# One raw PSUM tensor with up to three score slots, one bit group for both halves of a block, and new priorities

## The chip, the core and the metric

The kernel runs on one core of one Trainium2 chip (trn2). The metric is the device time of one execution in microseconds (us). The profile's span is about 2 us shorter in most runs, and 4 us shorter in the run that the prediction was made from, because it goes from the first to the last instruction. Fast and slow executions are kept apart; every comparison here is between fast runs, and every profile line that is quoted comes from a profile of the fast state.

## The reference

Hash attention over 32 heads (batch 4, 8 heads, 768 positions, head size 64), then a channel mix on the joined heads.

```python
# attention: positions see each other only if their 6 hash bits agree
q_bits = einsum('bhsd,dk->bhsk', q, proj) > 0          # the same for k
mask   = q_bucket[..., :, None] == k_bucket[..., None, :]
attn   = softmax(where(mask, q @ k.T / sqrt(64), -1e9))
x      = (attn @ v), heads joined to [4, 768, 512]
# channel mix with a shift by one position
xk = mu_k * x + (1 - mu_k) * x_prev                    # xr with mu_r
k  = relu(xk @ w_k) ** 2                               # 512 -> 1024
out = sigmoid(xr @ w_r) * (k @ w_v)                    # 1024 -> 512
```

## The kernel before

The kernel works on 16 blocks, each a pair of heads. A block goes through these steps:

- SyncE (SP) issues the loads of q, k and v.
- VectorE (DVE) splits q and k into a high and a low half-precision part.
- A transposing DMA turns them. For the first two blocks TensorE (PE) does this.
- TensorE forms six bucket bits for each position.
- VectorE reads the signs, and four small DMAs ("rows") lay the bits beside q and k as extra rows.
- Nine steps of scores, 128 x 1024 each, go through PSUM to ScalarE (ACT), which takes the exp.
- Attention times v follows, then the normalisation on VectorE, a transpose and the shift mix.

After every four blocks a batch is complete and its channel mix can run (groups KP, R and V below). From block 4 on, v is centred: GpSimd (POOL) sums it and a small "mean" matmul follows.

All work is entered in a list with an estimated duration, a priority and its dependencies. A planner in Python then simulates five engines and a DMA queue, and picks at each moment the ready operation of the lowest priority number. The order that comes out is fixed in the program. Each engine goes through its list in that order; a trace below shows an engine standing 3.0 us at one instruction while the ones behind it wait. The priorities count in blocks: an operation of block n has priority n + PR[name].

```python
LAG = {"PE": 0.30, "ACT": 0.25, "DVE": 0.20, "POOL": 0.20, "SP": 1.8, "GQ": 2.0}   # us, the planner's own numbers
PR = {
    'ldq': -2.811, 'ldv': -2.337, 'hi': -5.393, 'lo': -1.084, 'tr': -2.122, ...   # 34 numbers
    'va': 0.273, 'vsum': -2.003, 'mean': -0.515, ...
}
class Plan:
    def schedule(self):            # (cut) list scheduling
        ...
                    if o.take is not None:
                        cls, name, moe = o.take
                        if not avail[cls] or (moe and moe_held[cls] >= self.slots[cls][1]):
                            skipped.append(item)      # no PSUM slot free by the plan: try another
                            continue
        ...
# PSUM: two score slots of two banks, four small slots of one bank
sc_t = [psum.tile([P, STEP], FP32, name=f"sc{i}", tag=f"sc{i}") for i in range(2)]     # STEP = 1024
sm_t = [psum.tile([P, 512], FP32, name=f"sm{i}", tag=f"sm{i}") for i in range(4)]
plan = Plan({"sc": (2, 2), "sm": (4, 3)})
...
for h in range(2):                 # bits of a block: two groups of 384 columns, one small slot each
    def f(nm=nm, h=h):
        ps = sm(nm)
        for w_, st in ((p1, True), (p2, False)):
            for i in its:          # q and k of two heads, on four column strips
                nc.tensor.matmul(ps[32 * i : 32 * i + 32, 0:HALF], w_, a[:, i // 2, h * HALF : (h + 1) * HALF],
                                 start=st, stop=not st)
    def g(nm=nm, h=h):             # VectorE takes the sign bits
        nc.vector.tensor_scalar(out=bx_t[sx][lo_p:P, h * HALF : (h + 1) * HALF].bitcast(U16), in0=sm(nm)[...], ...)
```

The softmax here doesn't subtract the row's maximum and nothing guards it: scores larger than these inputs give would overflow.

## Time and profile before

The kernel took 260.83 us (two runs, 260.77 and 260.90).

The lines below are the busy time of each engine and the page's 40 equal slices of the span, in tenths of busy time, for the kernel before.

```profile
PE 239.3 (93%) x2519; PEld 143.5 (56%) x2519; DVE 195.1 (76%) x391; ACT 185.5 (72%) x242; POOL 57.9 (23%) x98
...
PE   6768898888999999999999989999999999999994
```

The busy time by stretch, kernel before. The columns are the stretch, its length, then the busy time and the instruction count of each engine, the granted clock of TensorE, the share of the 16 DMA engines and the DMA rate.

```profile
16.00:32.00 16.00, 13.11 (x154) 7.36 (x154) 13.47 (x25) 10.90 (x13) 6.60 (x11) 0.89 0.85 152
48.00:64.00 16.00, 13.24 (x183) 8.63 (x181) 12.81 (x23) 14.14 (x16) 7.58 (x13) 1.00 1.04 172
...
80.00:96.00 16.00, 15.84 (x141) 8.36 (x139) 15.62 (x28) 10.52 (x15) 5.23 (x6) 1.00 0.67 165
112.00:128.00 16.00, 16.00 (x194) 9.64 (x191) 14.85 (x31) 13.26 (x17) 2.75 (x4) 1.00 0.87 249
```

There are two stages. Up to about 64 us TensorE has gaps, because no channel-mix matmul can start before the first batch's attention is done. After that, TensorE is busy for practically the whole of each stretch.

The waits of TensorE, kernel before (who waited for whom: us in total, times, longest):

```profile
PE sc L553 <- ACT pt L557: 4.5, 11, 0.7
PE sm L420 <- DVE qh L405: 1.3, 1, 1.3
PE sm L443 <- DVE ak L422: 1.3, 2, 0.7
...
PE sm L681 <- DVE ob L599: 1.1, 1, 1.1
...
PE sm L609 <- DVE ob L599: 0.3, 1, 0.3
```

The largest is 4.5 us, scores waiting for a slot that exp has not yet emptied. Two more lines of the kernel before are needed later (start, duration, what). The first is from SyncE's timeline, the issue of a load of v; the second is from the chain of work in order of time, GpSimd's first sum of that v.

```profile
47.90 0.40 SPq L339 DMA_DIRECT2D vn<-in_v_dram  x1
```

### The profile page before, as it was taken

The page shows a single profiled execution, that of the slowest core. Times are in us where ns is not written, and L with a number is a line of the kernel's source. Part 1 is how long each engine was busy: PE and PEld are TensorE (multiplying, and loading weights), DVE is VectorE, ACT ScalarE, POOL GpSimd, SP SyncE. Part 2 cuts the span into 40 slices and gives each one's busy share as a digit, 9 for nine tenths or more (in the row PEclk, how much of TensorE's full clock was granted, in tenths as well). Part 3 has the DMA queues.
Part 4 walks back from the last instruction along what each step waited for, and adds up shares of the span by engine and source line. Part 5 has one row for each costly group of instructions (what it writes and reads, how often), then busy time and mean ns, then how long its engine had stood idle before and what let it go on. Part 6 is the DMA issues. An engine that isn't in the chain of part 4 may idle for free.

```text
span 256.8 us, 6319 instructions
## 1 busy us (share of the span) xinstructions
PE 239.3 (93%) x2519; PEld 143.5 (56%) x2519; DVE 195.1 (76%) x391; ACT 185.5 (72%) x242; POOL 57.9 (23%) x98
## 2 busy tenths in 40 slices
PE   6768898888999999999999989999999999999994
PEld 2334564555666456656666655555666666555441
DVE  4999676777789997989998999898685753675322
ACT  3838888888994598878898967586798986147320
POOL 2491415056051330504041424040000000000000
PEclk9998999999999999999999999999999999999999
DMA  6968979799998479796978987888200011220132
GB/s 191 382 168 155 163 174 172 199 171 180 225 201 227 116 199 175 212 241 190 274 148 266 216 241 149 233 164 166 89 3 6 3 41 43 82 86 1 41 123 82
DMA packets 64565, 39.78 MB, mean 155 GB/s; under 512 B 46756, under 2 KB 60952, under 8 KB 64536
## 3 DMA queue, kind: packets, MB, share of 16 engines
q1 hardware_dynamic: 62248, 36.76, 58.4%
q0 software_dynamic: 2208, 2.62, 6.3%
q8 instruction: 19, 0.31, 0.5%
q14 instruction: 10, 0.08, 0.1%
q10 hardware_dynamic: 80, 0.00, 0.0%
HBM read 24.12 MB, written 6.29 MB: 118 GB/s over the span
## 4 chain that ended last, share of the span: by engine, by line
PE 63%; DMA 15%; DVE 10%; POOL 3%; SPq 3%; issue 2%; ACT 2%; POOLq 0%; DVEq 0%
PE sc L553 16%; PE sm L681 15%; PE sm L652 11%; PE sm L583 10%; DMA vn<-in_v_dram 8%; PE sm L671 7%; PE sm L443 4%; DMA qn<-in_q_dram 3%; DMA ak<-kh 2%; POOL vt L360 2%; DMA kn<-in_k_dram 2%; PE sm L609 2%; ACT pt L557 2%; SPq L334 1%; DVE xk L635 1%
## 5 line engine op out<-in xcount | busy, mean ns | idle before, releaser
L557 ACT ACTIVATE pt<-sc 128x1024 bf16<-128x1024 f32 x144 | 143.2, 1028 | 29.9 <-PE sc L553 28.3
L553 PE MATMUL sc<-aq,ak 128*128 128x512 f16 (+1 forms) x384 | 84.6, 329 | 4.5 <-ACT pt L557 4.5
L553 PEld LDWEIGHTS <-ak 128*128 128x128 f16 x384 | 33.6, 98 | 31.1 <-issue 12.2
L652 PE MATMUL sm<-xk,wk 128*128 128x384 bf16 x256 | 48.9, 326 | 0.2
L681 PE MATMUL sm<-wv,k 128*128 128x512 bf16 x192 | 47.8, 379 | 1.1 <-DVE ob L599 1.1
L583 PEld LDWEIGHTS <-pt 128*128 128x128 bf16 x1152 | 42.9, 97 | 9.0 <-issue 0.6
L583 PE MATMUL sm<-va,pt 128*128 128x65 bf16 x1152 | 44.6, 193 | 0.0
L656 ACT ACTIVATE kr<-sm 128x384 bf16<-128x384 f32 x64 | 31.3, 498 | 9.5 <-PE sm L652 7.5
L652 PEld LDWEIGHTS <-wk 128*128 128x128 bf16 x256 | 24.1, 98 | 15.2 <-issue 0.3
L360 POOL TENSOR_TENSOR vt<-vn 128x384 f32<-128x384 f32 x12 | 15.1, 1256 | 71.5 <-DMA vn<-in_v_dram 71.5
L659 DVE TENSOR_TENSOR k<-kr 128x384 bf16<-128x384 bf16 x64 | 23.8, 385 | 8.5 <-ACT kr L656 8.4
L674 ACT ACTIVATE rs<-sm 128x512 f32<-128x512 f32 x24 | 14.4, 599 | 22.1 <-PE sm L671 18.9
L681 PEld LDWEIGHTS <-k 128*128 128x128 bf16 x192 | 18.4, 98 | 19.5 <-issue 1.3
L688 DVE SCALAR_TENSOR_TENSOR os<-rs,sm 128x512 f32<-128x512 f32 x24 | 16.3, 684 | 16.5 <-PE sm L681 16.4
L671 PE MATMUL sm<-wr,xr 128*128 128x512 bf16 x96 | 24.6, 379 | 0.0
L619 POOL COPY xt<-xt 128x127 bf16<-128x127 bf16 x16 | 8.4, 525 | 69.1 <-DVE xt L615 64.4
L447 DVE TENSOR_SCALAR bx<-sm 128x384 uint16<-128x384 uint16 (+1 forms) x32 | 16.4, 549 | 3.3 <-PE sm L443 2.6
L599 DVE TENSOR_TENSOR ob<-sm,rc 128x384 bf16<-128x384 f32 x32 | 17.8, 556 | 0.9
L405 DVE SCALAR_TENSOR_TENSOR kh<-kn,kh 128x768 f16<-128x768 f32 x15 | 18.3, 1219 | 0.1
L635 DVE SCALAR_TENSOR_TENSOR xk<-df,muk,xt 128x768 bf16<-128x768 bf16 x16 | 16.7, 1046 | 0.3
L443 PE MATMUL sm<-ak,p 128*32 128x384 f16 x124 | 14.4, 335 | 2.3 <-DVE ak L422 1.3
L635 DVE SCALAR_TENSOR_TENSOR xr<-df,mur,xt 128x768 bf16<-128x768 bf16 x16 | 16.1, 1018 | 0.0
(76 smaller groups left out, 195.3 us busy)
## 6 DMA issues: line engine op xcount, KB each, us to landing
vn<-in_v_dram SPq DMA_DIRECT2D x16, 384.0 KB
out_dram<-os SPq DMA_DIRECT2D x24, 256.0 KB
qn<-in_q_dram SPq DMA_DIRECT2D x15, 384.0 KB
kn<-in_k_dram SPq DMA_DIRECT2D x15, 384.0 KB
wk<-in_moe_w_k_dram POOLq DMA_DIRECT2D x4, 256.0 KB, 5.3
wv<-in_moe_w_v_dram POOLq DMA_DIRECT2D x4, 256.0 KB, 8.7
wr<-in_moe_w_r_dram POOLq DMA_DIRECT2D x2, 256.0 KB, 5.4
aq<-bx SPq DMA_DIRECT2D x31, 9.0 KB
```

Of the source, the lines that this page charges most:

```text
L360: nc.gpsimd.tensor_tensor(out=vt[:, :, :, 0:E], in0=src[:, :, 0:3, 0:E], in1=src[:, :, 3:6, 0:E], op=ALU.add)
L405: nc.vector.scalar_tensor_tensor(out=nh[:, :, D:P], in0=nat.rearrange("p j (c d) -> p (j c) d", d=D), scalar=QS, in1=nh[:, :, 0:D], op0=AL ...
L443: nc.tensor.matmul(ps[32 * i : 32 * i + 32, 0:HALF], w_, a[:, i // 2, h * HALF : (h + 1) * HALF], start=st, stop=not st)
L553: nc.tensor.matmul(ps[:, lo - s * STEP : hi - s * STEP], side_a["k"][sa][:, j, jc * P : (jc + 1) * P], side_a["q"][sa][:, j, q0 : q0 + hi ...
L557: nc.scalar.activation(out=pt_t[sp][:, s * STEP : (s + 1) * STEP], in_=sc_t[plan.slot[nm]], func=AF.Exp, bias=EBIAS, scale=ESC)
L583: nc.tensor.matmul(oo[:, ic * 65 : ic * 65 + 65], pt_t[sp][:, o : o + P], va_t[sa][:, j, jc, 0 : D + 1], start=(not uc and ic == 0 and jc ...
L635: nc.vector.scalar_tensor_tensor(out=dst[smx], in0=df_t[sd], scalar=mu[:, t : t + 1], in1=x, op0=ALU.mult, op1=ALU.add)
L652: nc.tensor.matmul(ps[:, 0:HALF], wk_sb[:, d, fc * P : (fc + 1) * P], xk_t[mx[d]][:, h * HALF : (h + 1) * HALF], start=(d == 0), stop=(d = ...
L656: nc.scalar.activation(out=kr_t[sk], in_=sm(nm)[:, 0:HALF], func=AF.Relu, scale=0.5 ** 0.5)
L659: nc.vector.tensor_tensor(out=k2_t[s2][:, h * HALF : (h + 1) * HALF], in0=kr_t[sk], in1=kr_t[sk], op=ALU.mult)
L671: nc.tensor.matmul(sm(nr), xr_t[mx[d]][:, c * P : (c + 1) * P], wr_sb[:, d, :], start=(d == 0), stop=(d == NDC - 1))
L681: nc.tensor.matmul(sm(nv), k2_t[(b * NFC + fc) % NK2][:, c * P : (c + 1) * P], wv_sb[:, fc, :], start=(fc == 0), stop=(fc == NFC - 1))
```

## The change

The intent is to give out more freely the eight banks into which the kernels divide PSUM. Scores may use up to three two-bank slots when the banks allow it. The bits of a whole block become one group in a two-bank slot, so that VectorE reads them in one pass. The 34 priorities are all new as well.

```diff
+    def __init__(self, pairs, banks, most, moe_most):
...
+        def room(take):
+            cls, _, moe = take
+            if count[cls] >= self.most[cls] or (moe and count["moe"] >= self.moe_most):
+                return None
+            if cls == "sc":
+                for i in self.pairs:
+                    if not used[2 * i] and not used[2 * i + 1]:
+                        return i, (2 * i, 2 * i + 1)
+                return None
+            for b in self.banks:
+                if not used[b]:
+                    return b, (b,)
+            return None
...
-    psum = ctx.enter_context(tc.tile_pool(name="ps", bufs=1, space=bass.MemoryType.PSUM))
+    ps_all = ctx.enter_context(nc.psum_tensor("ps_all", [P, 4 * STEP], FP32))
...
-    plan = Plan({"sc": (2, 2), "sm": (4, 3)})
+    ps_t = [ps_all[:, i * STEP : (i + 1) * STEP] for i in range(4)]
+    plan = Plan((0, 1, 2), (7, 6, 5, 4), {"sc": 3, "sm": 4}, 3)
...
-        for h in range(2):                       # bits: two groups, two reads
+            for w_, st in ((p1, True), (p2, False)):
+                for lo, hi in ((0, 512), (512, S)):
                     for i in its:
+                        nc.tensor.matmul(ps[32 * i : 32 * i + 32, lo:hi], w_, a[:, i // 2, lo:hi], start=st, stop=not st)
+        add("PE", 2 * MM(S) + 0.2, pb + PR["bits"], f, ..., take=("sc", nm, 0), name=nm)
+        add("DVE", DVE_C(S), pb + PR["bx"], g, r=[(nm,)], w=[("bx", sx)], give=[nm], name=f"bx{n}")
...
-    'ldq': -2.811, 'ldv': -2.337, 'hi': -5.393, 'lo': -1.084, 'tr': -2.122, 'bits': -1.224, 'bx': -4.393, 'row': 4.034,
-    'va': 0.273, 'vsum': -2.003, 'mean': -0.515, 'pv0': 0.767, 'pv1': 1.128, 'fin': -1.916, 'ot': 1.215, 'xt': -1.326,
+    'ldq': -4.096, 'ldv': -2.786, 'hi': -4.393, 'lo': -1.809, 'tr': -9.712, 'bits': -6.189, 'bx': -3.768, 'row': 6.869,
+    'va': -3.785, 'vsum': 5.153, 'mean': -1.211, 'pv0': 0.763, 'pv1': 1.093, 'fin': -0.954, 'ot': -2.354, 'xt': 0.515,
     (18 more numbers, all new)
```

The new tensor ps_all has 4 x 1024 fp32 columns for each partition, and the planner counts them as eight banks of 512. So three score slots use six banks and leave two for small groups, and the four small slots can only all be held while scores hold two.

## The prediction

> **What bounds the kernel now.** The span is 256.8 us, the reported time 260.83. Busy time by stretch shows two stages. From 64 us on TensorE is the limit: 15.8 to 16.0 of every 16 us (14.9 in 144 to 160); after 66 us its waits are one of 1.1 us (on DVE, at 149 us). Before 64 us it has 10.9, 13.1, 14.6 and 13.2 of 16. There ScalarE sets the pace: no channel-mix matmul can start before batch 0's four head pairs are through, and 45 exps stand before the first ReLU. Back to back an exp takes 0.97 us, so 45 need 43.7 us; in the ScalarE timeline they span 10.5 to 64.7 us, so ScalarE idles 10.5 us: 5.7 us in the first steps (head 1's bucket bits come back by DMA; the largest gap is 3.9 us, at 20.2 us), about 5 us in eleven gaps of 0.2 to 1.0 us later. About 2 us of these follow bit matmuls that wait for transposing DMAs (0.8 us each at 44 and 58 us); about 3 us are hand-over jitter with two score slots (scores wait for exp 4.5 us in all, and exp for scores).
>
> **What the change does.** No arithmetic goes. The instruction order shows 16 bit matmuls for a block before and after (4 groups of 384 columns become 2 of 512 and 2 of 256). VectorE reads the bits in one 128x768 pass instead of two 128x384 of 549 ns. [...] one pass should take about 950 ns and save 0.15 us x 15 = 2.2 us of VectorE (76% busy, mostly off the chain). The bit group takes one two-bank score slot, not two of the four small slots. Scores may hold three two-bank slots when the small ones leave banks 4 and 5 free. I found no new wait between different banks. The priorities, hence the whole order, are new.
>
> **What is on the critical path.** In the first stage the third slot lets TensorE run a step further ahead; I expect 2 of the 3 us of jitter back. The start is a wash: three score steps now precede the transposes, but VectorE reads head 1's bits later (behind two copies), so the fifth step should still start near 19 us. The DMA supply (mostly 0.8 to 1.15 of 16 engines until 176 us) caps the gain. In both orders 45 score steps and 4.5 blocks of attention-value work precede the first channel-mix matmul; about 182 us of matmul streaming remain from there, which neither slots nor VectorE shorten; perhaps 0.5 us of stalls go.
>
> **Prediction:** 258.8 us, range 256.4 to 261.2. Faster by over 2%: 0.06; within 2%: 0.91; slower by over 2%: 0.03.
>
> **What would show it.** The first channel-mix matmul starts at 61.5 us instead of 63.4; ScalarE's gaps between 20 and 64 us add up to about 3 us, not 5; scores' wait for exp falls below 3 us; the bit read lasts 0.95 us; TensorE stays about 16 of 16 us busy from 64 us, and the stretch from first channel-mix matmul to the end stays 193 us.
>
> **What would make it wrong.** The new order could starve TensorE in the saturated stage (two small slots left when scores hold three), or land transposes late; or remove the 3.9 us gap at 20 us, which would bring over 2%.

## More of the kernel before

```profile
51.92 1.00 POOL vt L360
```

The mean matmul of this block starts at 59.6 us, 11.7 us after the load was issued. Over the twelve blocks that have one, that distance is 7.1 to 34.5 us before the change.

## The result, and the profile after

The changed kernel took 270.48 us (270.31 and 270.64): slower, with a ratio of 1.041 (95% interval 1.033 to 1.049). A ratio in this text is the record's own ratio of fast runs, with its interval. It is not quite the ratio of the medians (1.037 here) or of the means in the table below; so a few tenths of a per cent between such figures mean nothing.

The lines below are the busy time and the slices, changed kernel.

```profile
PE 240.8 (90%) x2499; PEld 146.0 (54%) x2519; DVE 193.0 (72%) x375; ACT 185.7 (69%) x242; POOL 56.0 (21%) x98
...
PE   6966899399789999978899899996999999999994
```

The work did not grow. TensorE's busy time is 1.5 us longer and VectorE's is 2.1 us shorter (2.2 were predicted; how little that proves is said below). TensorE's idle time is what grew: span less busy time is 256.8 - 239.3 = 17.5 us before and 268.5 - 240.8 = 27.7 us after. The slices show where. There is a 3 at the eighth slice, then 7s and 8s where the kernel before has 9s.

Busy time by stretch, changed kernel (columns as above):

```profile
16.00:32.00 16.00, 11.25 (x143) 6.58 (x143) 14.12 (x22) 10.29 (x11) 6.86 (x11) 1.00 0.78 149
48.00:64.00 16.00, 11.50 (x133) 7.72 (x133) 10.44 (x20) 10.35 (x12) 5.12 (x8) 0.79 0.73 131
...
80.00:96.00 16.00, 15.66 (x176) 9.56 (x176) 13.01 (x27) 13.86 (x21) 4.84 (x7) 1.00 1.00 193
112.00:128.00 16.00, 13.84 (x120) 7.61 (x121) 10.70 (x21) 9.86 (x12) 5.52 (x7) 1.00 0.88 236
```

The first channel-mix matmul starts at 66.3 us (63.4 before), so 2.9 us are lost before it. From there to the end it takes 268.5 - 66.3 = 202.2 us against 256.8 - 63.4 = 193.4 us, so 8.8 us are lost after it, in the stage that was saturated before. The first and last start of its matmuls, and then the two stretches with their busy time; in each pair the kernel before comes first:

```profile
L652 PE MATMUL sm<-xk,wk x256: 322/326/326, 63.4 to 237.1; 128*128 128x384 bf16 x128
L668 PE MATMUL ps_all<-xk,wk x256: 322/326/337, 66.3 to 248.9; 128*128 128x384 bf16 x128
...
63.40:256.80 193.40, 188.12 (x1889) 112.66 (x1887) 146.59 (x300) 138.09 (x189) 32.59 (x43) 1.00 0.58 141
66.30:268.50 202.20, 187.82 (x1871) 112.76 (x1889) 145.10 (x292) 138.85 (x190) 34.61 (x49) 1.00 0.59 139
```

TensorE is busy for the same 188 us in both. Its idle time in this stage grew from 5.3 to 14.4 us, and that is the whole loss there.

The waits of TensorE, changed kernel:

```profile
PE ps_all L396 <- POOL vs L383: 6.1, 6, 1.6
PE ps_all L625 <- DVE ob L615: 4.1, 1, 4.1
PE ps_all L569 <- DMA ak<-bx: 3.1, 3, 1.3
PE ps_all L668 <- DVE xk L651: 1.6, 1, 1.6
...
PE ps_all L569 <- ACT pt L573: 1.0, 2, 0.7
```

The last line is what the third slot was meant to do: scores (L569) wait 1.0 us for exp, not 4.5. But three waits head the list that the kernel before hardly had. The mean matmul (L396) waits for GpSimd's sums of v, the output transpose (L625) for the normalisation on VectorE, and scores for the bit rows.

The wait of 4.1 us can be followed in the order of time. In the changed kernel's timeline of VectorE and TensorE the last bracket is the idle time before a line and what ended it.

```profile
48.27 0.56 DVE L419 TENSOR_SCALAR kh<-kn 128x768 f16<-128x768 f32 x1 [3.01 <-DMA kn<-in_k_dram]
...
51.57 0.56 DVE L615 TENSOR_TENSOR ob<-ps_all,rc 128x384 bf16<-128x384 f32 x1
...
52.19 0.82 PE L625 MATMUL ps_all<-idb,ob 128*128 128x128 bf16 x6 [4.14 <-DVE ob L615]
```

VectorE stands for 3.0 us at the conversion of a k that has not landed. The normalisation that TensorE needs comes behind it in the list. The k itself is hardly later than before: the kernel before converts its k at 48.64 us. But there the second normalisation of the block stands in front of the last conversion (49.10 us), and more scores stand in front of the transpose. The clock then drops; the stretches of 4 us around it, changed kernel:

```profile
48.00:52.00 4.00, 0.05 (x1) 0.00 (x0) 3.70 (x7) 2.14 (x3) 2.25 (x3) 0.83 0.44 114
52.00:56.00 4.00, 3.81 (x28) 2.62 (x29) 3.05 (x7) 1.91 (x2) 2.88 (x6) 0.50 1.10 187
56.00:60.00 4.00, 3.65 (x47) 2.57 (x46) 1.67 (x4) 2.69 (x4) 0.00 (x0) 0.82 1.14 186
```

The granted clock was still 1.00 in the first 2.6 us of the wait, 0.50 from 50.65 to 57.45 us, and 1.00 again after that; the table gives the same length, 2 x (0.17 + 0.50 + 0.18) x 4 = 6.8 us. In the kernel before it was 0.50 from 18.25 to 21.65 us, after 3.4 us in which TensorE had been busy for 1.7 us and had waited at most 0.7 us at a time. What sets the clock back is not shown by these runs. Here more was lost than the wait of 4.1 us: the six transposing matmuls behind it took 0.82 us at a granted clock of 0.50, against 0.50 us at 1.00 at 50.03 us in the kernel before.

The wait at the mean matmul is a chain from SyncE. The chain of work of the changed kernel in order of time (start, duration, what), with the block whose v the kernel before issued at 47.90 us:

```profile
68.52 3.79 DMA vn<-in_v_dram
...
72.45 1.01 POOL vt L377
...
74.35 0.42 POOL vs L383
...
74.81 0.22 PE ps_all L396
```

The load is issued 20.6 us later than before, and the mean matmul stands only 6.3 us behind it. For eleven of the twelve blocks that distance is now 5.5 to 10.3 us. Load and sums alone take 6.3 us in these lines, so the slack is nearly gone. A short distance alone is no loss, though: the kernel before has blocks with 7.1 and 8.4 us and no wait at the mean.

### The profile page after: what moved, and what is told of

Read it like the earlier page. It is cut to its first block, busy times and chain, and to the rows that moved or that the text cites. A ratio compares the mean times of both kernels' runs of the same rounds, so it can differ in the third digit from the quotient of the medians.

```text
span 268.5 us, 6301 instructions
## 1 busy us (share of the span) xinstructions
PE 240.8 (90%) x2499; PEld 146.0 (54%) x2519; DVE 193.0 (72%) x375; ACT 185.7 (69%) x242; POOL 56.0 (21%) x98
## 4 chain that ended last, share of the span: by engine, by line
PE 60%; DMA 21%; DVE 8%; POOL 5%; issue 3%; SPq 2%; ACT 0%; DVEq 0%; POOLq 0%; ACTq 0%
PE ps_all L569 15%; PE ps_all L697 12%; PE ps_all L668 11%; DMA vn<-in_v_dram 10%; PE ps_all L599 10%; PE ps_all L687 5%; DMA kn<-in_k_dram 4%; DMA ak<-kh 4%; POOL vt L377 3%; PE ps_all L460 3%; PE ps_all L625 2%; DMA aq<-qh 2%; DMA qn<-in_q_dram 1%; DVE qh L422 1%; POOL vs L383 1%
## 5 line engine op out<-in xcount | busy, mean ns | idle before, releaser
L573 ACT ACTIVATE pt<-ps_all 128x1024 bf16<-128x1024 f32 x144 | 141.2, 1027 | 33.7 <-PE ps_all L569 32.9
L569 PE MATMUL ps_all<-aq,ak 128*128 128x512 f16 (+1 forms) x384 | 81.6, 330 | 5.7 <-DMA ak<-bx 3.1
L668 PE MATMUL ps_all<-xk,wk 128*128 128x384 bf16 x256 | 48.5, 326 | 1.8 <-DVE xk L651 1.6
L569 PEld LDWEIGHTS <-ak 128*128 128x128 f16 x384 | 33.6, 98 | 29.1 <-issue 6.9
L599 PE MATMUL ps_all<-va,pt 128*128 128x65 bf16 x1152 | 46.5, 194 | 0.1
L697 PE MATMUL ps_all<-wv,k 128*128 128x512 bf16 x181 | 46.0, 379 | 0.5
L672 ACT ACTIVATE kr<-ps_all 128x384 bf16<-128x384 f32 x64 | 30.8, 495 | 17.7 <-PE ps_all L668 16.3
L690 ACT ACTIVATE rs<-ps_all 128x512 f32<-128x512 f32 x24 | 14.4, 599 | 20.6 <-PE ps_all L687 18.3
L704 DVE SCALAR_TENSOR_TENSOR os<-rs,ps_all 128x512 f32<-128x512 f32 x24 | 16.4, 681 | 16.7 <-PE ps_all L697 13.5
L687 PE MATMUL ps_all<-wr,xr 128*128 128x512 bf16 x87 | 23.5, 379 | 0.7 <-DVE os L704 0.3
L615 DVE TENSOR_TENSOR ob<-ps_all,rc 128x384 bf16<-128x384 f32 x32 | 17.8, 555 | 0.7
L422 DVE SCALAR_TENSOR_TENSOR qh<-qn,qh 128x768 f16<-128x768 f32 x15 | 15.9, 1063 | 0.1
```

What stands on the lines that cost most here:

```text
L422: nc.vector.scalar_tensor_tensor(out=nh[:, :, D:P], in0=nat.rearrange("p j (c d) -> p (j c) d", d=D), scalar=QS, in1=nh[:, :, 0:D], op0=AL ...
L569: nc.tensor.matmul(ps[:, lo - s * STEP : hi - s * STEP], side_a["k"][sa][:, j, jc * P : (jc + 1) * P], side_a["q"][sa][:, j, q0 : q0 + hi ...
L573: nc.scalar.activation(out=pt_t[sp][:, s * STEP : (s + 1) * STEP], in_=ps_t[plan.slot[nm]], func=AF.Exp, bias=EBIAS, scale=ESC)
L599: nc.tensor.matmul(oo[:, ic * 65 : ic * 65 + 65], pt_t[sp][:, o : o + P], va_t[sa][:, j, jc, 0 : D + 1], start=(not uc and ic == 0 and jc ...
L615: nc.vector.tensor_tensor(out=ob_t[so][:, :, j * D : (j + 1) * D], in0=oo[:, :, 0:D], in1=rc_t[sr][:, 1, :].unsqueeze(2).to_broadcast([P, ...
L668: nc.tensor.matmul(ps[:, 0:HALF], wk_sb[:, d, fc * P : (fc + 1) * P], xk_t[mx[d]][:, h * HALF : (h + 1) * HALF], start=(d == 0), stop=(d = ...
```

## The experiments

The theories tested were these:

- A: the new priorities, that is the order, cost the time.
- B: the new use of PSUM costs the time.
- C: the order of the kernel before is a selected one, and almost any other order loses.
- D: late transposing DMAs make the difference.
- E: the waits named above are themselves the lost time. F: they only show a lateness from elsewhere.

Eighteen kernels ran, each beside the kernel before on the same chip; all but the two marked "wrong" gave correct results. The changed kernel itself ran in the first rounds only, so a later run is compared with it across rounds, through the ratios to the kernel before. new_load_old and new_mean_late have two fast runs each, and the profiles of these two, of old_nudge1 and of new_loads_early are of the slow state. Fast runs only:

| run | mean us | before, same rounds | ratio (95% interval) |
|---|---|---|---|
| new_old_prio: new PSUM, old priorities | 272.0 | 259.3 | 1.049 (1.046 to 1.052) |
| old_new_prio: old PSUM, new priorities | 268.0 | 259.3 | 1.034 (1.029 to 1.038) |
| new_v_old: changed, v path's priorities old | 269.0 | 259.3 | 1.037 (1.033 to 1.042) |
| new_load_old: changed, q and k preparation old | 266.6 | 259.3 | 1.028 (1.023 to 1.033) |
| raw_only: before, on a raw PSUM tensor | 259.2 | 258.7 | 1.003 (0.994 to 1.011) |
| old_nudge1: before, priorities nudged | 267.6 | 258.7 | 1.036 (1.027 to 1.044) |
| old_nudge2: the same, other numbers | 268.4 | 258.7 | 1.039 (1.032 to 1.045) |
| new_nudge1: changed, priorities nudged | 275.3 | 258.7 | 1.065 (1.058 to 1.073) |
| order_old_merged: before's order, merged bits | 262.7 | 259.2 | 1.012 (1.005 to 1.018) |
| order_old_merged3: the same, third score slot | 266.2 | 259.2 | 1.027 (1.019 to 1.034) |
| old_plain_copy: before, no transposing DMA (wrong) | 254.8 | 259.2 | 0.983 (0.977 to 0.989) |
| new_plain_copy: changed, the same (wrong) | 266.2 | 259.2 | 1.027 (1.019 to 1.034) |
| old_v_early: before, loads of v earlier | 273.8 | 259.9 | 1.053 (1.045 to 1.061) |
| old_loads_early: before, loads of q, k, v earlier | 279.4 | 259.9 | 1.075 (1.067 to 1.082) |
| new_v_early: changed, loads of v earlier | 276.5 | 259.9 | 1.064 (1.055 to 1.072) |
| new_loads_early: changed, loads of q, k, v earlier | 288.6 | 259.9 | 1.110 (1.103 to 1.118) |
| new_mean_late: changed, mean matmuls later | 272.4 | 259.0 | 1.052 (1.044 to 1.060) |
| new_mean_hi_late: the same, and one k later on VectorE | 272.7 | 259.0 | 1.053 (1.046 to 1.060) |

### Priorities and structure crossed

The edits exchange the table PR between the two kernels; the planner then makes a new order for each.

```diff
# new_old_prio: changed kernel          # old_new_prio: kernel before
-PR = { ...the new 34 }                 -PR = { ...the old 34 }
+PR = { ...the old 34 }                 +PR = { ...the new 34 }
```

> The changed kernel (one raw PSUM tensor, up to three score slots, bits of both halves in one group) with the 34 priorities of the kernel before. Theory A (the loss comes from the new priorities, i.e. from the order of work): 258 to 261 us, ratio to before 0.99 to 1.00, and TensorE waits for GpSimd's sums of v at the mean matmul fall from 6.1 us to under 1 us. Theory B (the loss comes from the PSUM structure: banks shared by scores and small groups, bits taking a score slot): 267 to 271 us, ratio 1.03 or more.

> The kernel before with the priorities of the changed kernel, PSUM as before. Theory A: 267 to 273 us, ratio 1.03 or more, with TensorE waiting for GpSimd's sums and for VectorE again. Theory B: 260 to 263 us. If both this and the crossed run are slow, the priorities and the structure only work in pairs.

Both were slow, 1.049 and 1.034. Neither theory A nor theory B alone predicts that. The new priorities cost 3.4% without any change of PSUM, and the old ones do not bring the new structure back. Old priorities in the new structure still make a new order, since the planner finds other slots free at other times. So these two runs change the order in both cases, and leave open why a new order is bad. They also fit the third reading, that table and structure only work in pairs.

### Parts of the priorities put back

```diff
# new_v_old: changed kernel, six numbers as before
+    'ldv': -2.337, 'va': 0.273, 'vsum': -2.003, 'mean': -0.515, 'va_u': 2.059, 'vsum_u': -3.477,
# new_load_old: changed kernel, four numbers as before
+    'ldq': -2.811, 'hi': -5.393, 'lo': -1.084, 'tr': -2.122,
```

> The changed kernel with only the six priorities of the v path (load of v, its sums, the mean matmul, the centred v) as before. Theory A1 (the mean matmul stands too early on TensorE's queue against the load of v): the wait of TensorE for GpSimd falls from 6.1 to under 2 us, time 263 to 266 us. If the v path only takes the blame for a later block of work: no gain, 269 to 271 us.

> The changed kernel with only the four priorities of the q and k preparation (load, high part, low part, transposing DMA) as before. Theory A2 (loads of q and k issued late hold VectorE in order at 45 to 48 us and so TensorE at 48 to 52 us, 4.1 us): that wait goes, time 265 to 268 us; the waits for GpSimd's sums stay near 6 us. If the preparation order is not the cause: 269 to 272 us.

The first gave 269.0 us on average, no clear gain over the changed kernel (1.037 against 1.041). The waits for GpSimd did leave the list of TensorE's waits, and the output transpose waited 7.4 us for VectorE instead. The second has only two fast runs (265.8 and 267.4 us): 1.028, some 1.3% better than the change. That is short of half the loss, but it is inside the 265 to 268 us that theory A2 gave. Its profile is of the slow state and does not confirm the reason: the waits for GpSimd, which were to stay near 6 us, are not among those of 0.8 us and more there, and TensorE waits up to 3.6 us at a time for VectorE's read of the bits instead. Neither run puts the whole loss on one group of priorities.

### Is the raw tensor, or any new order, to blame?

```diff
# raw_only: kernel before, same slots, same order on every engine (compared instruction by instruction)
-    sc_t = [psum.tile([P, STEP], FP32, ...) for i in range(2)]
-    sm_t = [psum.tile([P, 512], FP32, ...) for i in range(4)]
+    sc_t = [ps_all[:, i * STEP : (i + 1) * STEP] for i in range(2)]
+    sm_t = [ps_all[:, 2 * STEP + i * 512 : 2 * STEP + (i + 1) * 512] for i in range(4)]
# old_nudge1, old_nudge2, new_nudge1: every priority + uniform(-0.05, 0.05), for instance
-    'ldq': -2.811, 'ldv': -2.337, 'hi': -5.393, 'lo': -1.084,
+    'ldq': -2.848, 'ldv': -2.302, 'hi': -5.367, 'lo': -1.108,
```

> The kernel before with the same two score slots and four small slots, cut out of one raw PSUM tensor instead of six pool tiles; the order of instructions on every engine is that of before. If the raw tensor costs nothing by itself (dependencies exact by bank): within 0.5% of before, 258.5 to 261 us. If it brings waits between different banks: 265 us or more.

> The kernel before with every one of the 34 priorities moved by a random amount of at most 0.05 (of a head pair's time); nothing else. Theory C (the order of the kernel before is a selected one, and almost any other order loses several us to in-order queues stuck behind late DMA): 263 to 271 us, ratio 1.015 or more. Rival (orders near it are as good; the order of the change is bad for a reason of its own): 259 to 262 us.

> As the first nudge of the kernel before, with other random numbers. Theory C: 263 to 271 us, not the same as the first nudge. Rival: 259 to 262 us.

> The changed kernel with every priority moved by a random amount of at most 0.05. Theory C: anything from 264 to 274 us, that is, as wide a spread around the changed kernel's 270.5 us as around the kernel before, mostly on its slow side only for before. Rival: within 1% of 270.5 us.

The raw tensor is free: 1.003, within its interval of 1. The nudges are the main finding, with a limit given below. Moving all priorities of the kernel before by at most a twentieth of a block costs 3.6% and 3.9%, as much as the new priorities (3.4%) and nearly as much as the whole change (4.1%). Theory C holds for the kernel before in both nudges that were tried. The one nudge of the changed kernel costs a further 2.3% (1.065 / 1.041); at 275.3 us it is slower than both of its expectations.

The limit was the planner's own end of each plan. Run alone afterwards, without the chip, the planners in the kernels end at 248.9 us for the kernel before and 247.9 us for the changed one, but at 255.4 and 252.4 us for the two nudges, 252.3 us for new_nudge1, 251.3 us for old_new_prio and 253.2 us for new_old_prio. So in the plan each of the two kernels already has a table that suits its own bank rules, and 3.5 to 6.5 us of the nudges' 9 to 10 us are lost in the plan. The nudges show what an order that suits its rules less costs. They do not show why the changed kernel, planned 1.0 us shorter, ran 9.7 us longer; that gap between plan and chip stays open.

The waits of TensorE in the second nudge of the kernel before show the same kind of thing as the change does, in a kernel with the old PSUM and nearly the old priorities:

```profile
PE sc L552 <- ACT pt L556: 6.2, 16, 0.7
PE sm L608 <- DVE ob L598: 4.6, 4, 2.0
PE sc L552 <- DMA ak<-bx: 1.8, 1, 1.8
```

The output transpose waits 4.6 us for VectorE and scores 1.8 us for the bit rows. The kernel before lists neither wait above 0.3 us in the profile quoted above. A caution belongs here: raw_only, which has the order of the kernel before and no loss, shows waits of 2.0 and 1.9 us of the same two kinds in its profiled run, the slowest of its four (261.63 us). A wait of 2 us in one profile is therefore no proof of a bad order; the loss over the rounds is.

### The new structure in the old order

To test the structure without a new order, the planner ran as in the kernel before, and the banks were then found for the fixed order by a search. ScalarE, GpSimd and SyncE have the same instructions in the same order, and so have TensorE and VectorE apart from the bits.

```diff
-    order = plan.schedule()
+    order = plan.schedule()                       # slots and priorities of the kernel before
+    give_banks(order, bank, npairs)               # 2: scores on two pairs; 3: on three
...
             def f(nm=nm, h=h):
+                if h == 0:
+                    return                        # the place of the first half stays empty
+                ps = ps_t[bank[nm]]               # both halves, in the place of the second
+                for w_, st in ((p1, True), (p2, False)):
+                    for lo, hi in ((0, 512), (512, S)):
```

> The order of the kernel before on every engine, with the change's merged bit group (both halves of a block written by one matmul group to two neighbouring banks and read by one VectorE pass) and the raw tensor; scores keep two slots, banks are found for the fixed order. Theory C (the loss is the order, the structure is harmless): 256.5 to 260 us, VectorE about 2 us less busy. If merging the bits costs time by itself (row DMAs later, banks shared): 263 us or more.

> As the run with the order of before and merged bits, but the scores go round three two-bank slots where two neighbouring banks are free (19 of 144 steps use the third). Theory C: 256 to 260 us, and the scores' waits for exp fall from 4.5 us to under 3.5 us. If sharing banks 4 and 5 between scores and small groups stalls TensorE: 262 us or more.

The merged bits alone cost 1.2%, not the hoped gain of VectorE's 2 us; 262.7 us lies between the two expectations. With the third slot it is 2.7%. The two intervals nearly touch, the two profiled runs have the same span (263.0 and 263.1 us), and the second run's search also ranks the banks for scores by another rule. So the size and the cause of the second step are uncertain; that the third slot brings no gain here is clear. The waits of TensorE with the third slot (L491 are the bits, L602 the scores):

```profile
PE ps_all L491 <- ACT pt L606: 4.4, 4, 1.8
...
PE ps_all L602 <- ACT pt L606: 0.5, 2, 0.4
```

Scores wait 0.5 us for exp instead of 4.5, so the slot does its work. The bits now wait 4.4 us for exp, in four waits, because they need two banks that a score step had. In the kernel before the bits never waited for ScalarE; with merged bits and two score slots they waited 1.4 us. The wait moved from scores to bits; how much slack either has was not measured. Theory B is true in this part: in an order planned for other slots, the new bank use costs 1 to 3%.

### Are late transposing DMAs the difference?

```diff
-    nc.sync.dma_start_transpose(out=a.rearrange("p j (c q) -> p (j c) q", q=P), in_=nh.rearrange("p c d -> p (c d)"))
+    nc.sync.dma_start(out=a.rearrange("p j (c q) -> p (j c) q", q=P), in_=nh)
```

> The kernel before, with each of its 28 transposing DMAs replaced by a plain DMA copy of the same bytes in the same place of the queue (wrong result on purpose, same order[...]). Theory D (the orders differ in how well they hide late DMA): before gains little, 253 to 259 us, because its order already hides the DMA. If before is itself held by DMA: under 250 us.

> The changed kernel with its 28 transposing DMAs replaced by plain copies of the same bytes (wrong result on purpose, same order). Theory D: most of its 10 to 12 us loss goes, 256 to 262 us, within 1.5% of the same edit of the kernel before, and waits for GpSimd's sums of v fall below 2 us. Rival (the order itself is too serial, whatever the DMA): 266 us or more.

Theory D falls. Without transposes the kernel before gains 1.7% and the changed kernel is at 1.027 instead of 1.041, so both gain some 4 us. The gap between them stays: 266.2 / 254.8 = 1.045. The changed kernel still waits as long for GpSimd at the mean matmul:

```profile
PE ps_all L396 <- POOL vs L383: 5.8, 6, 2.0
```

### Loads moved forward in SyncE's queue

Here the order of everything but the loads stays, on every engine. A load from block 4 on is put where, by the plan, its buffer has just become free: 16 to 35 places earlier for the changed kernel's loads of v.

```diff
-    order = plan.schedule()
+    order = hoist(plan.schedule(), [f"ldv{n}" for n in range(4, NPAIRS)], 0.0)     # new_v_early, old_v_early
+    order = hoist(plan.schedule(), [f"ld{x}{n}" for n in range(4, NPAIRS) for x in "vqk"], 0.0)   # ..._loads_early
```

> The changed kernel with its own order on every engine, but each load of v from block 4 on stands some 20 places earlier in SyncE's queue, as soon as its buffer is free by the plan. Theory E (late loads in SyncE's in-order queue stall TensorE through the chain load of v, sums on GpSimd, mean matmul): the waits of TensorE for GpSimd's sums fall from 6.1 us to under 1 us, and the time to 263 to 266 us. Rival (these waits are filled by others): 268 us or more.

> As the run with v loaded early, with the loads of q and k moved forward too. Theory E: VectorE's waits for loads of q and k (12.1 us in all) fall below 4 us, the 4.1 us wait of the output transpose for VectorE near 50 us goes, and the time is 259 to 263 us. Rival: 266 us or more.

> Control: the kernel before with its loads of v moved forward in SyncE's queue. TensorE waits there for no load of v, so theory E expects no gain: 257.5 to 261 us. If earlier loads help whatever the order: under 256 us.

> Control: the kernel before with its loads of q, k and v moved forward in SyncE's queue. VectorE waits only 4 us for loads there and TensorE hardly, so theory E expects 256 to 261 us.

All four were far slower than theory E expected; only the open-ended ranges of the rivals hold the two runs of the changed kernel. In new_v_early the waits for GpSimd's sums are gone, as theory E said, and the time rose from 1.041 to 1.064. The controls show that the edit itself is costly: old_v_early is 5.3% slower than the kernel before. First a wait of SyncE, then one of TensorE, in old_v_early:

```profile
SPq L353 <- DVE va L399: 16.8, 8, 4.3
```

```profile
PE sm L457 <- DMA ak<-kh: 8.3, 2, 7.0
```

SyncE stood 16.8 us at the loads of v (L353), waiting for VectorE to finish with their buffers. In the kernel before that is 1.2 us. The transposing DMAs behind them in SyncE's list were late, and the bit matmuls (L457) waited up to 7.0 us for one, against 0.5 us in the kernel before. That the one wait led to the other is inferred from the order of SyncE's list; these two lines do not show it. A load that was moved forward "as soon as its buffer is free by the plan" was moved to where the chip was not ready, and SyncE stood there with the rest of its list behind it. An early load is not a safe load where one queue issues loads and transposes in order: here it cost 5.3%, and 7.5% with q and k moved as well.

### The waits removed without touching SyncE

```diff
-    order = plan.schedule()
+    order = mean_later(plan.schedule(), plan, range(NUC, NPAIRS), 5.0, rep)   # up to 5 us later, bank by search
+    order = after_ob(order, "lo5", "ob2")       # new_mean_hi_late only: k of block 5 behind the
+    order = after_ob(order, "hi5", "ob2")       # normalisation of block 2 on VectorE
```

> The changed kernel, same order and banks of all else, but 9 of the 12 mean matmuls (with their VectorE readers) stand 3 to 5 us later by the plan, two others 0.4 and 0.9 us. Theory E (the waits at the mean matmul are time lost): waits of TensorE for GpSimd's sums fall from 6.1 to under 1.5 us, time 264 to 267 us. Theory F (they only show a lateness from elsewhere, which comes up at the next wait): the waits fall as much, but the time stays 268.5 us or more.

> As the run with late mean matmuls, and the high and low parts of k of block 5 stand behind both normalisations of block 2 on VectorE. Theory E: the 4.1 us wait of the output transpose near 50 us goes as well; 2 to 4 us faster than the run with late mean matmuls, 261 to 264 us. Theory F: within 1.5 us of it.

Again the waits went and the time did not. In new_mean_hi_late no wait of TensorE for GpSimd is left. These take its place (L622 scores, L721 the first channel-mix group, L462 VectorE's last reader of the mean):

```profile
PE ps_all L622 <- DVE mc L462: 4.7, 3, 2.7
...
PE ps_all L721 <- DVE mc L462: 1.8, 2, 1.1
```

This edit was not clean. The search put seven of the twelve mean groups on bank 4 and one on bank 5, the two halves of the third score slot, where the changed kernel has a single one (on bank 5); the scores then waited for those banks. So the runs do not decide between E and F for the mean matmul. They do show once more what sharing banks 4 and 5 does. For the other wait one profile speaks for theory E: with the one k moved, the output transpose near 50 us starts at 48.61 us without a wait, and the first channel-mix matmul at 64.0 us instead of 66.3. But the run as a whole (1.053) is no faster than its partner (1.052), so by its times the expectation of theory F was met.

## Why the prediction was wrong

- **What bounds the kernel: right.** Two stages, ScalarE's exps setting the pace of the first and TensorE saturated in the second. This is read from the profile before; no run tested it.
- **VectorE's read of the bits: right in its duration.** The predicted duration, the author's estimate, was 950 ns. The group's mean is 953 ns in the profile after, where two reads of 549 ns stood before. VectorE's total is no test. It fell by 195.1 - 193.0 = 2.1 us, against a predicted 2.2, but raw_only and old_nudge2, which still make two reads, show 193.8 and 192.6 us; that agreement is luck. In the old order this saving bought nothing (1.012).
- **The raw tensor: right.** raw_only shows no new kind of wait and is at 1.003.
- **The start: right.** ScalarE resumes after its large gap at 19.57 us, 20.20 before.
- **The third slot: its mechanism right, its worth wrong.** Scores' wait for exp fell from 4.5 to 1.0 us (predicted: below 3). But ScalarE's gaps between 20 and the first ReLU grew from 5.1 to about 9 us instead of shrinking to 3, the first channel-mix matmul came at 66.3 us instead of 61.5, and in the old order the waits only moved from scores to bits.
- **The step that failed** is in the section on the critical path: "about 182 us of matmul streaming remain from there, which neither slots nor VectorE shorten; perhaps 0.5 us of stalls go." It took the saturated second stage for a property of the work. It is a property of one order. The stretch from the first channel-mix matmul to the end was predicted to stay at 193 us and took 202.2 us, 8.8 of the 11.7 us by which the span grew. The streaming itself did not change (TensorE busy 188.1 us before, 187.8 after). The term that was wrong is the stalls: 0.5 us were to go, and 9.1 us came (5.3 us idle before, 14.4 after). The prediction had noted that the priorities, "hence the whole order, are new", and priced that at nothing. The nudges show what price an order can have: 3.6 and 3.9% for one that differs by a twentieth of a block in its priorities. Why this new order, which the planner put 1.0 us ahead, stalls on the chip is not shown.
- **What was not looked at** was at hand before the run. The comparison of the orders counted the work before the first channel-mix matmul on TensorE and ScalarE, where both agree. It did not compare the distance, along SyncE, GpSimd and TensorE, between a load of v and the mean matmul that needs it. The new table moves 'vsum' from -2.003 to 5.153 and 'mean' from -0.515 to -1.211, which is a reason to look. In the trace this distance is 7.1 to 34.5 us before and 5.5 to 10.3 us after for eleven of twelve blocks. That this distance cost the time is not shown: new_v_early and new_mean_late took the waits away and were slower.
- **The alternative was named and undervalued.** "The new order could starve TensorE in the saturated stage" is what happened; it had been given a chance of 3%.

What stays open: how much of the 4.1% belongs to the order and how much to the banks does not add up from these runs (1.034 for the priorities alone, 1.012 to 1.027 for the banks alone in the old order, 1.049 for the new banks with the old priorities). Which feature makes the old order good was not found: taking away single waits gave no time back in new_v_old, new_v_early, new_mean_late and new_mean_hi_late, and new_load_old, which won 1.3%, has no fast profile to say why. Whether priorities chosen on the chip for the new banks would reach the old time was not tried. No version beat the kernel before with a correct result.

## What to carry to other kernels

Where a planner fixes the order and the chip runs it in order, a change that makes the planner plan again is first of all a change of order. Nudge the old kernel's priorities once or twice to learn what another order can cost (here 3.6 to 3.9%), look at the planner's own end of each plan to see how much of it is planned, and test the structure itself with the order held fixed.

A wait that heads the list is where the lateness shows. Before counting it as a gain, ask what stands behind the instruction that would be moved: in a queue that issues loads and transposes in order, loads moved forward cost 5.3 to 7.5% in a kernel that had no such wait. And a buffer shared by two kinds of work can hand a wait from one to the other: here scores' wait for exp fell to 0.5 us and the bits' rose to 4.4 us. Which of them has slack has to be measured first; here it was not.
